# A planned attention and feed-forward kernel: loads and turns dealt out by a clock of the transfers, and the last products in other banks

## The chip, the cores and the metric

The kernel runs on one core of one Trainium2 chip. The metric is the device time of one execution in microseconds (us). The engines are named as in the profile: PE is TensorE (matmuls), PEld its weight loads, DVE is VectorE, ACT is ScalarE, POOL is GpSimd, SP is SyncE, which only issues transfers; ACT and POOL can issue them too. PSUM, where matmuls write, has eight banks.

## What is computed

```python
# q: (8, 16, 384, 64)   k, v: (8, 4, 384, 64)   w_in: (1024, 2048)   w_out: (2048, 1024)
k, v = repeat(k, 4, axis=1), repeat(v, 4, axis=1)
scores = q @ k.T / sqrt(64)
attn = exp(scores - max(scores)); attn = attn / (sum(attn) + 1e-9)
x = (attn @ v).transpose(0, 2, 1, 3).reshape(8 * 384, 1024)
out = (maximum(x @ w_in, 0) ** 2) @ w_out                  # (3072, 1024), float32
```

Grouped-query attention over eight batches feeds a feed-forward layer with a squared ReLU. One batch of attention gives the 384 rows of `x` on which the feed-forward of that batch works.

## The kernel before

The whole kernel is written by a planner that runs when the program is built. The class `Recorder` takes every operation with its engine, what it reads and writes, and a cost in us, and keeps a planned clock for each engine (`R.clock`) and a planned end for each operation. Two loops then choose, step by step, the next piece of work for TensorE among the candidates (`sc` scores, `av` attention times values, `ffn` the next piece of the feed-forward, `top` small products that spread a maximum). The first loop runs until the feed-forward reaches batch `SB` = 2, the second one (batches 2 to 7) to the end. Nothing is decided on the chip: each engine gets its list in the order in which the planner recorded it, with semaphore waits for what the list needs.

The feed-forward of batch b runs beside the attention of batches b+1 and b+2. From batch 2 on, both matrix products are done by Strassen's scheme with seven products in place of eight. The up-projection is in `strassen` (matmuls of 192 columns, L921); its operands are sums of quarters of `x`, made by `sums` on VectorE (L676, four additions of 16-bit values for a batch, kept in the queue `lazy`). The results are drained by `evict` (L892 to L905), and `close_squares` squares them on ScalarE or GpSimd (L806 to L818). The output products are in `products` and `pair_of` (matmuls of 512 columns, L963); their operand sums are in `sum_ops` (L1201), the drains in `copied` and `added` (L1114 and L1121), and one sum of two results is taken on GpSimd (L1153). Pieces that use half of the rows of the array are laid side by side with `zipped`, so two matmuls of 64 rows run at a time. The list of banks for these pieces is `order`, which starts as `[4, 5, 6, 7]` and is permuted by each batch; attention uses banks 0 to 3. `strassen(b)` is built the first time that `whole(b)` is called.

Around TensorE's choice stands `upkeep(now)`, called before every choice. It hands out the work of the other engines in a written order of queues. What the change touches:

- `load_pieces`: the loads of keys and of four groups of query heads for a batch (L292, L327), issued by GpSimd.
- `chores`: per batch the doubling of the keys (`dup_k`, L356: on ScalarE when no list of feed-forward pieces is open, otherwise on GpSimd), the turn of the keys by a transposing transfer (`turn_k_half`, L373), the load of the values (L320), the turns of the queries (`turn_q_dma`, L380) and a copy of the values (`aug_v`, L362).
- `o_wait`: the turns of attention's output into `xT` (`turn_o_dma`, L553). All turns are issued by SP.
- `puts`: the output transfers (`send`, L1329), issued by SP.
- `lazy`, `d_q`, `wide_q`, `calm`, `w2_q`: operations of VectorE and others.

Loads and turns are paced: `dma_at` is the earliest planned time for the next one (`LOAD_GAP` = 2.0 us behind a load, `TURN_GAP` = 3.5 us behind a turn), and `calm_at(now)` looks at the count of matmuls so far, `R.tally.n`: with 128 matmuls to a block and an edge at count 51 of each, it lets a transfer go when the next edge is at least 1.5 us away and the last one at least 0.3 us behind, or when TensorE takes under 18 matmuls a us. Each paced transfer also waits on the chip for the latest matmul recorded before it (`gate`), so that it isn't issued early.

The last output product of the last batch, `whole_product`, is cut in two pieces of 384 and 128 columns; the last drain is split the same way, and `send` puts both on SP's queue.

Of the kernel before, what the change touches and what calls it, by code (L numbers as in the profile page):

```python
# [21 lines left out]
class Recorder:  # L22


    ENGINES = ("tensor", "scalar", "vector", "gpsimd", "sync")
    IN_ORDER = ("tensor",)

    def __init__(self, nc):
        self.nc = nc
        self.ops = []  # L30
        self.writer = {}
        self.readers = {}
        self.dma_sems = {}
# [5 lines left out]
        self.marks = []  # L39

    def deps_of(self, reads, writes):
        deps = set()
# [18 lines left out]
    def add(self, eng, fn, reads=(), writes=(), dma=None, cost=0.1, issue=0.1, shared=(), after=(), port=False):  # L61
        i = len(self.ops)
        deps = self.deps_of(reads, writes)
        raw = {self.writer[r] for r in reads if r in self.writer}
        for r in reads:
            self.readers.setdefault(r, []).append(i)
        for w in writes:
            self.writer[w] = i
            self.readers[w] = []
        need = set(after)  # L70
        for d in deps:
            o = self.ops[d]
            if o["dma"] is None and o["eng"] == eng and dma is None:
                if eng in self.IN_ORDER or d not in raw:
                    continue
            need.add(d)
        if dma is not None:
            if dma in self.dma_last:
                need.add(self.dma_last[dma])
            self.dma_last[dma] = i  # L80
        start = max([self.clock[eng]] + [self.ops[d]["end"] for d in need])
        if dma is not None:
            self.clock[eng] = start + issue
            if eng == "gpsimd":
                self.pool.append((start, start + 0.3 * issue))
            q = eng
            begin = max(self.ring.get(q, 0.0), start + issue + 0.8)
            if shared and begin > start + issue + 0.8:
                shared = (3.0, shared[1])
            if shared and self.ring.get("gpsimd", 0.0) > begin:  # L90
                self.ring["gpsimd"] += shared[1]
                for o in self.ops:
                    if o["eng"] == "gpsimd" and o["dma"] is not None and o["end"] > begin:
                        o["end"] += max(0.0, min(shared[1], o["end"] - 1.2 - begin))
                cost = shared[0]
            self.ring[q] = begin + cost
            end = begin + cost + (1.5 if begin > 30 else 1.2 if eng == "gpsimd" else 0.7)
        else:
            if eng == "gpsimd":
                self.pool.append((start, start + cost))  # L100
            elif port:
                cost += max([0.0] + [z - start for a, z in self.pool[-6:] if a <= start < z])
            self.clock[eng] = start + cost
            if eng == "tensor":
                fn(self.tally)
                self.marks.append((start + cost, self.tally.n))
            end = start + cost + (0.2 if eng == "tensor" else 0.07)
        self.ops.append(dict(eng=eng, fn=fn, dma=dma, need=need, signal=False, start=start, end=end))
        return i
# [57 lines left out]
def bass_gqa_attention__then__ffn_squared_relu_kernel(  # L167
# [12 lines left out]
    B, H, S, D = 8, 16, 384, 64  # L180
# [4 lines left out]
    NKC = F // 128  # L185
# [1140 lines left out]
    def send(b, i3, c0, c1, yb, y0=0):  # L1326
        ysl = y_sb[yb][:, y0:y0 + c1 - c0]
        rows = out[b * S:(b + 1) * S, :].rearrange("(p j) f -> j p f", j=NJ)[i3]
        put = lambda: R.add("sync", lambda e: e.dma_start(rows[:, c0:c1], ysl),  # L1329
                            reads=[("y", yb)], writes=[("out", b, i3, c0)], dma=f"y{yb}" + "z" * (y0 > 0), cost=0.6)  # L1330
# [108 lines left out]
    def prepare(b):  # L1439
# [4 lines left out]
        def go(turn, *args):  # L1444
            turn(b, *args, gate=tuple(pe_last) if paced else ())
            if paced:
                dma_at[0] = R.clock["tensor"] + TURN_GAP
            if turn is turn_q_dma:
                turned_h.add((b, args[0]))
            if turn is turn_q_dma and args == (1,):  # L1450
# [150 lines left out]

    def whole(b):
        if b not in built:
            built[b] = strassen(b, ff["carry"])
        return built[b]

# [37 lines left out]

    BLOCK, EDGE = 128, 51

    def calm_at(now):
        if ff["b"] < SB:
            return True
        n = R.tally.n  # L1650
        t, m = next((x for x in reversed(R.marks) if x[1] <= n - BLOCK // 2), R.marks[0])
        rate = (n - m) / (now - t)
        if rate < 18:
            return True
        left = (EDGE - n) % BLOCK / rate
        return 1.5 <= left <= BLOCK / rate - 0.3

    o_wait = []

    def turn_o_waiting():  # L1660
        while o_wait:
            b, g = o_wait.pop(0)
            turn_o_dma(b, g, tuple(pe_last))
            dma_at[0] = max(dma_at[0], R.clock["tensor"] + 3.5)
            x_done[b] += 2

    def upkeep(now):
        nonlocal loaded, queued, turned
        pe_last[0:1] = [len(R.ops) - 1 - next(i for i, o in enumerate(reversed(R.ops)) if o["eng"] == "tensor")]
        if o_wait and calm_at(now):  # L1670
            turn_o_waiting()
        if loaded + 1 < B and turned >= loaded and not turn_q and not load_pieces and not chores:
            loaded += 1
# [16 lines left out]
            else:  # L1690
# [5 lines left out]
        if load_pieces and now >= dma_at[0] and calm_at(now) and R.when(writes=load_pieces[0][0], reads=(load_pieces[0] + ((),))[2], eng="none") + 2.0 <= now:  # L1696
            load_pieces.pop(0)[1](tuple(pe_last[0:1]))
            dma_at[0] = now + LOAD_GAP
        if not chores and halves and (halves[0] - 1, NU - 1, 5) in scored and (halves[0] > LATE or x_done[halves[0] - 1] == NKC):
            prepare_rest(halves[0])  # L1700
        if not chores and not load_pieces and not halves and queued < loaded and (queued - (queued == 1), NU - 1 if queued + 1 < LATE else NU // 2 - 1, 5) in scored and pairs >= queued * 8 + 8 * (queued == 1) - 8 * (queued + 1 >= LATE):
            queued += 1
            prepare(queued)
        stretch[0] = split and ff["b"] < SB or bool(ff["now"])
        while chores and R.when(reads=chores[0][0], eng="none") + (chores[0] + (False, 0.0))[3 if len(chores[0]) > 3 else -1] <= now + margin and not (len(chores[0]) > 2 and chores[0][2] and (now < dma_at[0] or not calm_at(now))):
            chores.pop(0)[1]()
            if not chores and not halves:
                turned = queued
# [307 lines left out]
```

## Time and profile before

| | |
|---|---|
| Time, median of 3 runs | 399.15 us (398.44 to 399.24) |
| Profiled execution | 397.95 us, span 396.0 us |
| TensorE clock granted | 1.000 |
| TensorE busy | 388.1 us (98%), 7022 matmuls |
| VectorE busy | 316.3 us (80%) |
| ScalarE busy | 264.4 us (67%) |
| GpSimd busy | 151.1 us (38%) |
| Transfers | 44.39 MB, mean 112 GB/s |

The span runs from the first to the last instruction of the profiled execution; the time of that execution is 1.95 us longer. In the rows below, a time such as 298.76 is the start in us from the start of the span, the number behind it the duration; brackets give the idle time ahead of the instruction and what ended it. Line numbers are those of the kernel before; from the edits on, the changed kernel's are up to 13 higher.

### The profile page before, as it was taken

What the parts mean: (1) busy time and instruction counts of PE and PEld (TensorE: products, weight loads), DVE (VectorE), ACT (ScalarE), POOL (GpSimd) and SP (SyncE); (2) the same over time, 40 slices, a digit from 0 to 9 for tenths busy, and PEclk for the clock granted to TensorE, in tenths of its full rate; (3) what the DMA queues carried; (4) which work ended last, traced back from release to release, by engine and by line L of the source; (5) the groups of instructions that cost most, each with busy time, mean ns of one, the idle gap of its engine ahead of it and who ended that gap; (6) DMA issues with size and microseconds to landing.
All of it is one profiled execution on the core that took longest, in us unless ns stands there. A gap on an engine that the chain in (4) does not pass through costs nothing.

```text
span 396.0 us, 15645 instructions
## 1 busy us (share of the span) xinstructions
PE 388.1 (98%) x7022; PEld 292.1 (74%) x7022; DVE 316.3 (80%) x654; ACT 264.4 (67%) x384; POOL 151.1 (38%) x173
## 2 busy tenths in 40 slices
PE   8999999999999999999999999999999999999996
PEld 5565764455655998499876899799974799789653
DVE  3689879899989998878997888878897688856642
ACT  6948999688556796578728587868725597426511
POOL 8656410056002565068413263066420145126111
PEclk9999999999999999999999999999999999999999
DMA  9999999995229936659469957484476221120022
GB/s 171 175 199 187 207 186 192 180 221 82 41 77 141 163 49 83 109 123 102 64 112 190 139 89 73 89 149 58 65 107 167 79 45 25 46 84 3 28 81 106
DMA packets 95634, 44.39 MB, mean 112 GB/s; under 512 B 75984, under 2 KB 89552, under 8 KB 95568
## 3 DMA queue, kind: packets, MB, share of 16 engines
q0 software_dynamic: 36672, 17.44, 35.4%
q1 hardware_dynamic: 58224, 25.47, 32.1%
q8 instruction: 55, 0.90, 0.9%
q10 hardware_dynamic: 672, 0.49, 0.4%
q14 instruction: 11, 0.09, 0.1%
HBM read 35.65 MB, written 12.58 MB: 122 GB/s over the span
## 4 chain that ended last, share of the span: by engine, by line
PE 87%; DVE 7%; DMA 3%; POOL 1%; issue 1%; ACT 0%; ACTq 0%; DVEq 0%
PE ps L963 30%; PE ps L921 27%; PE ps L629 7%; PE ps L466 7%; PE ps L533 7%; PE ps L1297 5%; DMA wx<-in_q_dram 2%; PE ps L492 2%; DVE hr L642 1%; PE ps L592 1%; DMA wx<-in_k_dram 1%; DVE w_out_sb L1247 1%; DVE y_sb L1121 1%; DVE w_out_sb L1259 1%; DVE s_all L676 0%
## 5 line engine op out<-in xcount | busy, mean ns | idle before, releaser
L476 ACT ACTIVATE expT<-ps 128x1024 bf16<-128x1024 f32 (+1 forms) x124 | 121.1, 1017 | 37.6 <-PE ps L466 37.2
L963 PE MATMUL ps<-w_out_sb,h2T 64*128 64x512 f16 x528 | 96.3, 376 | 0.0
L921 PE MATMUL ps<-xT,w_in_sb 64*128 64x192 f16 x1152 | 84.2, 243 | 0.4 <-DVE y_sb L1121 0.3
L921 PEld LDWEIGHTS ps<-xT,w_in_sb 64*128 64x128 f16 x1152 | 71.4, 94 | 3.4 <-DVE y_sb L1121 0.5
L818 POOL TENSOR_TENSOR h2T<-hr 128x384 f16<-128x384 f32 x56 | 45.4, 832 | 45.6 <-ACT hr L806 45.4
L963 PE MATMUL ps<-area,xT 64*128 64x512 f16 x288 | 55.3, 376 | 0.0
L963 PEld LDWEIGHTS ps<-w_out_sb,h2T 64*128 64x128 f16 (+1 forms) x528 | 38.5, 94 | 19.0 <-ACT h2T L814 0.5
L921 PE MATMUL ps<-s_all,wx 64*128 64x192 f16 x768 | 51.8, 243 | 0.0
L466 PE MATMUL ps<-qT,kT 64*128 64x256 bf16 (+2 forms) x336 | 50.3, 323 | 0.9 <-ACT expT L476 0.6
L806 ACT ACTIVATE hr<-hr,bits 128x384 f32<-128x384 f32 x71 | 41.9, 608 | 10.1 <-DVE hr L905 9.5
L921 PEld LDWEIGHTS ps<-s_all,wx 64*128 64x128 f16 x768 | 44.4, 94 | 0.7
L905 DVE TENSOR_TENSOR hr<-ps,hr 128x384 f32<-128x384 f32 x72 | 39.2, 554 | 6.3 <-PE ps L921 2.5
L533 PE MATMUL ps<-v_aug,expT 64*128 64x65 bf16 x1680 | 43.9, 190 | 0.1
L1121 DVE SCALAR_TENSOR_TENSOR y_sb<-ps,bits,y_sb 128x512 f32<-128x512 f32 (+2 forms) x38 | 27.1, 723 | 20.4 <-PE ps L963 9.6
L629 PE MATMUL ps<-xT,w_in_sb 64*128 64x384 bf16 x448 | 41.9, 323 | 1.0 <-DVE hr L642 0.9
L533 PEld LDWEIGHTS ps<-v_aug,expT 64*128 64x128 bf16 x1680 | 39.9, 94 | 1.4 <-PE ps L533 0.2
L1114 ACT ACTIVATE y_sb<-ps,bits 128x512 f32<-128x512 f32 x20 | 13.6, 687 | 35.4 <-PE ps L963 35.4
L963 PE MATMUL ps<-area,h2T 64*128 64x512 f16 x144 | 36.2, 376 | 0.0
L1153 POOL TENSOR_TENSOR y_sb<-y_sb 128x512 f32<-128x512 f32 x9 | 11.9, 1320 | 62.7 <-DVE y_sb L1121 62.7
L629 PEld LDWEIGHTS ps<-xT,w_in_sb 64*128 64x128 bf16 x448 | 21.9, 94 | 16.2 <-DVE hr L642 2.2
L921 PE MATMUL ps<-xT,wx 64*128 64x192 f16 x384 | 33.0, 243 | 0.2 <-DVE hr L905 0.2
L921 PE MATMUL ps<-s_all,w_in_sb 64*128 64x192 f16 x384 | 32.7, 242 | 0.0
(147 smaller groups left out, 748.5 us busy)
## 6 DMA issues: line engine op xcount, KB each, us to landing
out_dram<-y_sb SPq DMA_DIRECT2D x45, 256.0 KB, 2.5
w_in_sb<-in_moe_w_in_dram POOLq DMA_DIRECT2D x8, 512.0 KB, 15.2
w_out_sb<-in_moe_w_out_dram POOLq DMA_DIRECT2D x4, 1024.0 KB, 28.4
q_st<-in_q_dram POOLq DMA_DIRECT2D x19, 192.0 KB, 4.9
q_st<-in_q_dram POOLq DMA_DIRECT2D x4, 384.0 KB, 23.5
k_st<-in_k_dram POOLq DMA_DIRECT2D x6, 192.0 KB, 4.5
k_st<-in_v_dram POOLq DMA_DIRECT2D x5, 192.0 KB, 3.8
wx<-in_q_dram POOLq DMA_DIRECT2D x2, 384.0 KB, 9.1
```

Of the source, the lines that this page charges most:

```text
L466: mm = pe.matmul(ps[:, base + x, m * wide:(m + 1) * wide], kT[at(b)][64 * x:64 * x + 64, u, :], q_cols(b, u // NJ, x, c0, c0 + wide))
L476: R.add("scalar", lambda e: e.activation(dst, src, AF.Exp, scale=0.125), reads=keys, writes=[("expT", slot(b, u), t) for u, _, _ in pieces ...
L533: m = pe.matmul(ps[:, p[x], n * DP:n * DP + D + 1], w, v_aug[b % 2][r, g * NJ + j, 0:D + 1], start=(n + j + y == 0), stop=(n + j + y == 2 ...
L629: m = pe.matmul(bank(4 + xs[x])[:, 0:S], w_in_sb[r, kc, c * 128:(c + 1) * 128], xT[b % NXT][r, kc, :], start=(phase < 2 and kc == 0), stop ...
L806: R.add("scalar", lambda e, val=val, to=to: e.activation(val, val, AF.Relu, scale=to), reads=[("hr", r)] + by, writes=[("hr", r)], cost=0. ...
L818: n = R.add(eng, lambda e, dst=dst, two=two: e.tensor_tensor(dst, two, two, ALU.mult), reads=[("hr", r)], writes=keys, cost=0.77 if other ...
L905: R.add("vector", lambda e: e.tensor_tensor(hr[r][:, :], src, hr[r][:, :], ALU.add), reads=[("bank", at), ("hr", r)], writes=[("hr", r)], ...
L921: return lambda pe: pe.matmul(bank(at)[:, f * h:f * h + h], w[r, kc, c:c + 128], m[r, kc, :], start=(prod in (1, 5, 2) and y + f + kc == 0 ...
L963: return lambda pe: pe.matmul(bank(p.at)[:, 0:512], p.a(k, r), p.w(k, r), start=start, stop=stop, skip_group_check=True)
L1114: R.add(eng, lambda e: e.activation(y_sb[y], bank(at), AF.Copy, scale=gs[g]) if eng == "scalar" else e.tensor_scalar(y_sb[y], bank(at), gs ...
L1121: R.add("vector", lambda e: e.scalar_tensor_tensor(y_sb[z][:, c0:c1], bank(at)[:, c0:c1], gs[g], y_sb[y][:, c0:c1], ALU.mult, ALU.add), re ...
L1297: m = pe.matmul(bank(i)[:, 0:n], h2T[:, c, i3 * 128:(i3 + 1) * 128], w_out_sb[:, c, c0:c1], start=(c == 0), stop=(c == NFC - 1))
```

## The change

A second clock, `R.wire`, is kept in `Recorder.add`: for each transfer, by its kind, a lag and an amount of work (`WIRE`; 2.2 and 1.25 us for a kind that isn't listed) are added up, so that it tells when the transfers given out so far are done. `calm_at` gets the kind of the next transfer and lets it go when the work with it would end less than 1.5 us behind the next edge of 128 matmuls, or, right at an edge, when little is under way; where TensorE takes under 18 matmuls a us, when it would end within 6 us. The fixed gaps behind a load and a turn become 0.5 us, and that behind a turn of attention's output 0, from batch 2 on.

`shut(now)` keeps the sums of `lazy` back while VectorE's next planned start falls into a pass of GpSimd. The sums of batch 3 are taken up earlier. For the last batch `order` is set to banks 0 to 3 before `strassen` is built. The last piece of 128 columns is sent from ScalarE's queue.

```diff
+    WIRE = dict(turn_q=(1.6, 1.9), turn_o=(0.8, 1.3), turn_k=(1.3, 1.3), y=(1.8, 0.8))
...
             self.ring[q] = begin + cost
+            kind = dma.rstrip("0123456789z_")
+            lag, work = self.WIRE.get(kind, (2.2, 1.25))
+            self.wire = max(self.wire, start + lag) + work
...
-        put = lambda: R.add("sync", lambda e: e.dma_start(rows[:, c0:c1], ysl),
+        put = lambda: R.add("scalar" if y0 else "sync", lambda e: e.dma_start(rows[:, c0:c1], ysl),
...
-                dma_at[0] = R.clock["tensor"] + TURN_GAP
+                dma_at[0] = R.clock["tensor"] + (TURN_GAP if ff["b"] < SB else 0.5)
...
     def whole(b):
         if b not in built:
+            if b == B - 1:
+                order[:] = [0, 1, 2, 3]
             built[b] = strassen(b, ff["carry"])
...
-    def calm_at(now):
+    def calm_at(now, kind):
         if ff["b"] < SB:
             return True
         n = R.tally.n
         t, m = next((x for x in reversed(R.marks) if x[1] <= n - BLOCK // 2), R.marks[0])
         rate = (n - m) / (now - t)
+        lag, work = R.WIRE.get(kind, (2.2, 1.25))
+        over = max(R.wire, now + lag) + work
         if rate < 18:
-            return True
+            return over <= now + 6.0
         left = (EDGE - n) % BLOCK / rate
-        return 1.5 <= left <= BLOCK / rate - 0.3
+        return (over <= now + left + 1.5 or left < 0.3 and R.wire <= now + 2.0) and left <= BLOCK / rate - 0.3
...
             turn_o_dma(b, g, tuple(pe_last))
-            dma_at[0] = max(dma_at[0], R.clock["tensor"] + 3.5)
+            dma_at[0] = max(dma_at[0], R.clock["tensor"] + 0)
...
+    def shut(now):
+        t = max(now, R.clock["vector"])
+        return ff["b"] >= SB and any(a <= t < z - 0.3 for a, z in R.pool[-6:])
...
-        if o_wait and calm_at(now):
+        if o_wait and calm_at(now, "turn_o"):
...
-            dma_at[0] = now + LOAD_GAP
+            dma_at[0] = now + (LOAD_GAP if ff["b"] < SB else 0.5)
...
-        while lazy and R.when(reads=lazy[0][0], eng="none") <= now + near and R.clock["vector"] <= now + near:
+        while lazy and R.when(reads=lazy[0][0], eng="none") <= now + near and R.clock["vector"] <= now + near and not shut(now):
...
-        if b and R.when(reads=[("xT", b % NXT, c) for c in range(NKC)], eng="none") + (3.3 if b > SB else 2.0) <= now + 0.3:
+        if b and R.when(reads=[("xT", b % NXT, c) for c in range(NKC)], eng="none") + (3.3 if b > SB + 1 else 1.0 if b > SB else 2.0) <= now + 0.3:
```

Since the planner chooses by its clocks, the lists of all engines come out in another order from batch 2 on. The matmuls are the same 7022, shape by shape. The start of TensorE's list, up to the first pieces of batch 2's up-projection, is unchanged.

More of the change, by code (lines that the diff above doesn't have):

```diff
@@ L39, in __init__ @@
         self.marks = []
+        self.wire = 0.0
     def deps_of(self, reads, writes):
@@ L1695, in upkeep @@
                     load_pieces.append(([("v_st", 0)], lambda g: load_v(n, g)))
-        if load_pieces and now >= dma_at[0] and calm_at(now) and R.when(writes=load_pieces[0][0], reads=(load_pieces[0] + ((),))[2], eng="none") + 2.0 <= now:
+        if load_pieces and now >= dma_at[0] and calm_at(now, "q") and R.when(writes=load_pieces[0][0], reads=(load_pieces[0] + ((),))[2], eng="none") + 2.0 <= now:
             load_pieces.pop(0)[1](tuple(pe_last[0:1]))
-            dma_at[0] = now + LOAD_GAP
+            dma_at[0] = now + (LOAD_GAP if ff["b"] < SB else 0.5)
         if not chores and halves and (halves[0] - 1, NU - 1, 5) in scored and (halves[0] > LATE or x_done[halves[0] - 1] == NKC):
@@ L1704, in upkeep @@
         stretch[0] = split and ff["b"] < SB or bool(ff["now"])
-        while chores and R.when(reads=chores[0][0], eng="none") + (chores[0] + (False, 0.0))[3 if len(chores[0]) > 3 else -1] <= now + margin and not (len(chores[0]) > 2 and chores[0][2] and (now < dma_at[0] or not calm_at(now))):
+        while chores and R.when(reads=chores[0][0], eng="none") + (chores[0] + (False, 0.0))[3 if len(chores[0]) > 3 else -1] <= now + margin and not (len(chores[0]) > 2 and chores[0][2] and (now < dma_at[0] or not calm_at(now, "turn_q"))):
             chores.pop(0)[1]()
```

## The prediction

> **What bounds the kernel now.** I read the head of the page first, then the chain, then the waits of TensorE, and last the timeline at each wait.
>
> ```profile
> span 396.0 us, 15645 instructions
> PE 388.1 (98%) x7022; PEld 292.1 (74%) x7022; DVE 316.3 (80%) x654; ACT 264.4 (67%) x384; POOL 151.1 (38%) x173
> PE 87%; DVE 7%; DMA 3%; POOL 1%; issue 1%; ACT 0%; ACTq 0%; DVEq 0%
> ```
>
> TensorE is busy for 388.1 of 396.0 us and holds 87% of the chain that ended last. Its list is the same 7022 matmuls in the changed program, of the same shapes, counted line by line. So the change can win only what TensorE idles, and the tail behind its last matmul; it can lose any amount. All planner edits are switched by `ff["b"] >= SB`, so they act once the feed-forward is at batch 2, from about 129 us. The waits of TensorE between 129 and 396 us, as total, times and longest:
>
> ```profile
> PE ps L963 <- DVE y_sb L1121: 0.6, 1, 0.6
> PE ps L921 <- DVE y_sb L1121: 0.3, 1, 0.3
> PE ps L466 <- ACT expT L476: 0.3, 1, 0.3
> PE ps L921 <- DVE hr L905: 0.2, 1, 0.2
> ```
>
> That is 1.4 us in four waits, and no releaser is a transfer. Hence the part that gives the change its name, earlier loads and turns, has no wait on TensorE to remove in this execution. What can be won hangs on VectorE's order.
>
> One correction. A matmul row outlasts the step to the next pair:
>
> ```profile
> L963 PE MATMUL ps<-w_out_sb,h2T 64*128 64x512 f16 x528 | 96.3, 376 | 0.0
> 156.13 5.18 PE ps L963 x48
> ```
>
> 48 half-array matmuls in 5.18 us are 24 pairs of 0.216 us each, while one row lasts 0.376. So a stall has eaten 0.16 us of lost pace before a gap shows: each wait above costs its idle time plus 0.16.
>
> **The change part by part.** First, sums out of GpSimd's passes. The largest wait, with what ran ahead of it on VectorE and GpSimd:
>
> ```profile
> 292.13 1.16 POOL L362 COPY v_aug<-k_st 128x768 bf16<-128x768 bf16 x1 [2.85 <-DMA k_st<-in_v_dram]
> 292.53 1.18 DVE L676 TENSOR_TENSOR s_all<-xT 128x768 f16<-128x768 f16 x1
> 295.30 0.74 DVE L1121 SCALAR_TENSOR_TENSOR y_sb<-ps,bits,y_sb 128x512 f32<-128x512 f32 x1
> 295.96 0.54 DVE L676 TENSOR_TENSOR xT<-xT 128x768 f16<-128x768 f16 x1
> 296.12 1.51 POOL L1153 TENSOR_TENSOR y_sb<-y_sb 128x512 f32<-128x512 f32 x1 [2.83 <-DVE y_sb L1121]
> 296.42 1.62 DVE L676 TENSOR_TENSOR s_all<-xT,s_all 128x768 f16<-128x768 f16 x1
> 297.97 0.74 DVE L1121 SCALAR_TENSOR_TENSOR y_sb<-ps,bits,y_sb 128x512 f32<-128x512 f32 x1
> 298.76 0.39 PE L963 MATMUL ps<-w_out_sb,area 64*128 64x512 f16 x1 [0.63 <-DVE y_sb L1121]
> ```
>
> The add at 296.42 lasts 1.62 us where its like lasts 0.54. It began inside GpSimd's pass, which ends at 297.63, and ends 0.41 behind it at 298.04; the add at 292.53 does the same against the pass that ends at 293.29. The add at 295.96 began 0.16 us ahead of the pass and kept its length. So an add that starts inside a GpSimd pass waits the pass out. The drain at 297.97 stands behind it, and TensorE waits for that drain's bank. In the changed order only one of the four sums stands between the two drains, not two: the lists read drain, add, add, drain before and add, drain, add, drain after. GpSimd's pass starts on the first drain's end, so the one add left begins ahead of it, as that of 295.96 did. The two lists hold the same four operations, so the second drain gains the stretch, 1.62 - 0.54 = 1.08 us, more than the 0.79 (0.63 + 0.16) that TensorE lost. Next late is the first drain, which now has an add of 0.54 ahead of it; its row shows no wait of a matmul behind it. I take the whole stall, **-0.79**; between 0 and -0.79.
>
> The Trainium skill, "SBUF — State Buffer", section "Who interferes with whom", says that a VectorE instruction with two SBUF inputs and a GpSimd instruction that reads SBUF block each other fully, whichever issues second waiting to the end. The three adds agree with that. By this rule GpSimd's own pass is held instead when the add is first; the trace has that too, 1.51 us at 296.12, and only an output transfer follows it.
>
> Second, the same collision with a copy that is moved.
>
> ```profile
> 136.79 1.46 POOL L356 COPY k_dup<-k_st 128x1536 bf16<-128x1536 bf16 x1
> 137.23 1.56 DVE L1259 TENSOR_TENSOR w_out_sb<-w_out_sb 128x1024 f16<-128x1024 f16 x1
> 138.72 1.01 DVE L905 TENSOR_TENSOR hr<-ps,hr 128x384 f32<-128x384 f32 x2
> 139.31 0.25 PE L921 MATMUL ps<-xT,wx 64*128 64x192 f16 x1 [0.24 <-DVE hr L905]
> L1259 DVE TENSOR_TENSOR w_out_sb<-w_out_sb x4: 677/1160/1559, 134.1 to 141.3; 128x1024 f16<-128x1024 f16 x4
> ```
>
> Here 1.56 us against a least of 0.68. The changed order puts this operation one drain of attention (reciprocal and multiply) earlier, so that the reciprocal and the multiply stand between it and the adds of L905. Whether the copy still meets it the order does not tell; between 0 and -0.40 (0.24 + 0.16), I take **-0.40**, because the adds of L905 no longer stand directly behind the long operation.
>
> Third, the last products in attention's banks (`order[:] = [0, 1, 2, 3]` for the last batch).
>
> ```profile
> 349.33 1.41 DVE L1121 SCALAR_TENSOR_TENSOR y_sb<-ps,bits,y_sb 128x512 f32<-128x512 f32 x2 [1.46 <-PE ps L921]
> 350.14 1.50 PE L921 MATMUL ps<-xT,w_in_sb 64*128 64x192 f16 x32 [0.28 <-DVE y_sb L1121]
> ```
>
> The first products of the last batch stop for a bank that a drain of the batch before still reads. Attention's banks 0 to 3 are long empty then. The drain of 349.33 stays but nobody waits for it: 0.28 + 0.16 = **-0.44**; next late there would be the vector sums, which stand before it in the list. I see little that takes it back.
>
> Fourth, the tail. The last piece of 128 columns goes out on ScalarE's queue instead of second on SP's.
>
> ```profile
> 393.08 0.35 DVE L1121 SCALAR_TENSOR_TENSOR y_sb<-ps,bits,y_sb 128x128 f32<-128x128 f32 x1
> 393.45 0.82 SPq L1329 DMA_DIRECT2D out_dram<-y_sb  x2
> out_dram<-y_sb SPq DMA_DIRECT2D x1, 192.0 KB, 1.9
> out_dram<-y_sb SPq DMA_DIRECT2D x1, 64.0 KB, 1.8
> L1329 SPq DMA_DIRECT2D out_dram<-y_sb x47: 332/333/1243, 75.7 to 393.8; - x47
> ```
>
> Both wait for the add that ends at 393.43. The 192 KB piece lands 1.9 us after 393.45, at 395.35; the 64 KB piece, issued 0.33 to 0.38 later, at about 395.6. Side by side, the first sets the end: **-0.25**; between 0 and -0.38. ScalarE has nothing behind that issue.
>
> Fifth, loads and turns by the transfer clock. No wait of TensorE is theirs, so nothing is taken out. What moves: four query loads in a row on GpSimd (they stood two, one, one between squares), turns of queries, keys and outputs back to back on SP, output transfers behind them. On GpSimd the squares wait behind up to four issues; SP's output transfers wait too, but y buffers come round after tens of us. Two key copies move from GpSimd to ScalarE, which is 67% busy:
>
> ```profile
> L1114 ACT ACTIVATE y_sb<-ps,bits 128x512 f32<-128x512 f32 x20 | 13.6, 687 | 35.4 <-PE ps L963 35.4
> L356 POOL COPY k_dup<-k_st 128x1536 bf16<-128x1536 bf16 x4 | 6.1, 1516 | 0.0
> PE ps L629 <- DVE hr L642: 0.9, 2, 0.7
> ```
>
> A copy of 1.5 us ahead of an exponential that TensorE needs could cost that much at worst. But the code gives it to ScalarE only outside a running list of pieces, among output products, and there ScalarE sat idle for 35.4 us behind L963 (the row of L1114), so I put it at nothing. But re-dealing the order of six batches will make some new wait. The nearest price is one small wait, 0.20 + 0.16 = **+0.36**; from 0 to two waits like the longest one of TensorE, 2 × (0.7 + 0.16) = 1.72.
>
> Sum: -0.79 - 0.40 - 0.44 - 0.25 + 0.36 = **-1.5**. The profiled execution took 397.95 us (1.95 around its span of 396.0), so 396.45; the median of the runs is 399.15, 1.2 above it, and by the same difference comes out at 397.65. I forecast **397.7**. A change within 0.2%, 0.8 us, is about what cannot be told from none.
>
> **The rivals.** *New waits take back what the old ones gave.* For it: VectorE is 80% busy, four small waits go and the order behind each is new, and the price above reaches 1.72. Against it: the two largest gains have a cause that is gone by construction (bank, add count). Then -1.88 + 1.72, about -0.2: 399.0, no difference.
>
> *Clumped turns delay TensorE's instructions; slower.* The page's queues:
>
> ```profile
> q0 software_dynamic: 36672, 17.44, 35.4%
> q1 hardware_dynamic: 58224, 25.47, 32.1%
> q8 instruction: 55, 0.90, 0.9%
> xT<-o_sb SPq DMA_TRANSPOSE x26, 3.1
> qT<-q_st SPq DMA_TRANSPOSE x12, 4.7
> kT<-k_dup SPq DMA_TRANSPOSE x11, 3.4
> 221.00:226.00 5.00, 5.00 (x175) 4.86 (x171) 4.73 (x10) 2.69 (x4) 0.67 (x1) 1.00 0.89 130
> ```
>
> 55 transfers bring 7022 matmuls and as many weight loads: one for 128 pairs. Each takes 0.9% × 16 × 396 / 55 = 1.04 us on one engine. At 175 matmuls in 5 us TensorE eats a block in 3.7 us, so a block that is late by over 3.7 - 1.0 = 2.7 us stops it. After the change output, key and query turn stand in a row three times, which never happened before; one behind the other they last 3.1 + 3.4 + 4.7 = 11.2 us. Against it: in 221 to 226 us a key turn, three output transfers, an output turn and a query load's tail overlapped, and TensorE was busy for 5.00 of 5.00. If a block waits out just what a query turn has over that block, 4.7 - 3.7 = 1.0, and the 1.04 of its own, three clumps cost 6.1 at worst and 3.1 with half: 397.65 + 3.1 = 400.8, slower. It decides from 2.7 us of delay.
>
> The Trainium skill, "DMA: Bandwidth & Descriptors", section "Queues, rings and completion order", has each DMA engine go round its queues packet by packet. By that rule a block waits for a packet or two of the others and never for a clump, and this rival is worth nothing; it would equally leave the transfer clock without use.
>
> **How the numbers follow.** The forecast, faster by more than 0.8 us, gets 0.68: three of four gains are seen in rows, and each alone is under the bound, so two must come. No difference gets 0.15. Slower gets 0.17: the clumps with most of it, the ScalarE copy with the rest. The forecast's own range goes from 396.0 (all gains, no new wait, -1.88, and some 1.2 for the runs lying nearer to the profiled one) to 398.3; with the same case and part of the slower one it reaches 400.4, and about one in ten lies beyond.
>
> **What would show it.** Right: in the waits of TensorE after 129 us the row with L963 behind the drain is gone, no L921 waits for a drain near 349 us, no sum of the last but one batches lasts over 1 us, and the last two transfers are issued side by side. Wrong: a new releaser of TensorE of over 0.5 us (an exponential behind a key copy, a drain behind a stretched sum), or steps with no releaser named in the stretches where turns stand three in a row, which would be its instructions. If all waits are gone and the time is the same, then the runs' 1.2 us above the profiled one hold something that this page does not show.

## The result and the profile after

| | before | after |
|---|---|---|
| Time, median | 398.88 us (398.00 to 400.00) | 396.16 us (395.66 to 397.23) |
| Profiled execution, span | 397.95 us, 396.0 us | 397.23 us, 395.4 us |
| First row of the stretch to the start of the last matmul | 129.77 to 392.55: 262.78 us | 130.92 to 391.92: 261.00 us |

The ratio of the times is 0.9935 (0.9913 to 0.9958): faster by 2.7 us. In the runs of the experiments the changed kernel took 395.68 us beside 397.99 before, 0.9937 (0.9918 to 0.9957). The last row of the table is the part that the change touches, from the first L921 (after: L926) behind a pair of scores to the start of the last matmul. The list of TensorE up to there is the same in both, and only its position in the span differs from execution to execution: this first row lay between 128.6 and 131.0 us in the profiles below. So comparisons of two traces go by this stretch. It is 1.78 us shorter.

The page after, its span and first part:

```profile
span 395.4 us, 15642 instructions
PE 388.7 (98%) x7019; PEld 295.8 (75%) x7022; DVE 312.0 (79%) x649; ACT 270.6 (68%) x394; POOL 144.7 (37%) x168
```

Three matmul records are missing from this trace, and from all those below; the 7022 weight loads are there. The waits of TensorE between 129 and 396 us (total, times, longest), where there were four with 1.4 us:

```profile
PE ps L471 <- DVE bits L712: 0.2, 1, 0.2
PE ps L926 <- DVE y_sb L1126: 0.2, 1, 0.2
```

The timeline of VectorE and GpSimd at the place where the longest wait was, now with one sum between the two drains:

```profile
296.99 0.55 DVE L681 TENSOR_TENSOR xT<-xT 128x768 f16<-128x768 f16 x1
297.61 0.75 DVE L1126 SCALAR_TENSOR_TENSOR y_sb<-ps,bits,y_sb 128x512 f32<-128x512 f32 x1
298.28 0.55 DVE L681 TENSOR_TENSOR s_all<-xT,s_all 128x768 f16<-128x768 f16 x1
298.44 1.51 POOL L1158 TENSOR_TENSOR y_sb<-y_sb 128x512 f32<-128x512 f32 x1 [13.31 <-DVE y_sb L1126]
299.55 0.75 DVE L1126 SCALAR_TENSOR_TENSOR y_sb<-ps,bits,y_sb 128x512 f32<-128x512 f32 x1 [0.73 <-PE ps L968]
```

The sum at 298.28 is ahead of the pass and keeps 0.55 us. The second drain now waits for TensorE (0.73 behind L968), not the other way round. One sum of another batch still meets a pass, the copy of L1225 that ends at 255.84, and ends 0.43 behind it:

```profile
254.27 2.00 DVE L681 TENSOR_TENSOR s_all<-xT 128x768 f16<-128x768 f16 x1
```

### The profile page after: what moved, and what is told of

Its sections match the earlier page's. It is cut to its first block, busy times and chain, and to the rows that moved or that the text cites. A ratio compares the mean times of both kernels' runs of the same rounds, so it can differ in the third digit from the quotient of the medians.

```text
span 395.4 us, 15642 instructions
## 1 busy us (share of the span) xinstructions
PE 388.7 (98%) x7019; PEld 295.8 (75%) x7022; DVE 312.0 (79%) x649; ACT 270.6 (68%) x394; POOL 144.7 (37%) x168
## 5 line engine op out<-in xcount | busy, mean ns | idle before, releaser
L968 PE MATMUL ps<-w_out_sb,h2T 64*128 64x512 f16 x528 | 98.1, 376 | 0.0
L926 PE MATMUL ps<-xT,w_in_sb 64*128 64x192 f16 x1152 | 83.8, 243 | 0.3 <-DVE y_sb L1126 0.2
L926 PEld LDWEIGHTS ps<-xT,w_in_sb 64*128 64x128 f16 x1152 | 70.7, 94 | 3.0 <-PE ps L926 0.7
L823 POOL TENSOR_TENSOR h2T<-hr 128x384 f16<-128x384 f32 x54 | 43.5, 826 | 55.6 <-ACT hr L811 55.6
L968 PE MATMUL ps<-area,xT 64*128 64x512 f16 x288 | 55.7, 376 | 0.0
L968 PEld LDWEIGHTS ps<-w_out_sb,h2T 64*128 64x128 f16 (+1 forms) x528 | 39.1, 94 | 17.7 <-ACT h2T L819 0.3
L471 PE MATMUL ps<-qT,kT 64*128 64x256 bf16 (+2 forms) x336 | 51.2, 327 | 0.6 <-ACT expT L481 0.4
L926 PE MATMUL ps<-s_all,wx 64*128 64x192 f16 x768 | 51.3, 242 | 0.0
L926 PEld LDWEIGHTS ps<-s_all,wx 64*128 64x128 f16 x768 | 44.1, 94 | 1.0
L538 PE MATMUL ps<-v_aug,expT 64*128 64x65 bf16 x1680 | 42.7, 190 | 0.0
L538 PEld LDWEIGHTS ps<-v_aug,expT 64*128 64x128 bf16 x1680 | 38.9, 94 | 1.5
L1119 ACT ACTIVATE y_sb<-ps,bits 128x512 f32<-128x512 f32 x23 | 15.6, 687 | 34.9 <-PE ps L968 34.7
L1158 POOL TENSOR_TENSOR y_sb<-y_sb 128x512 f32<-128x512 f32 x9 | 11.9, 1320 | 67.4 <-DVE y_sb L1126 67.4
L968 PE MATMUL ps<-area,h2T 64*128 64x512 f16 x144 | 35.9, 376 | 0.0
L634 PEld LDWEIGHTS ps<-xT,w_in_sb 64*128 64x128 bf16 x448 | 21.1, 94 | 16.8 <-DVE hr L647 2.2
L926 PE MATMUL ps<-xT,wx 64*128 64x192 f16 x384 | 32.9, 242 | 0.0
L926 PE MATMUL ps<-s_all,w_in_sb 64*128 64x192 f16 x384 | 32.2, 242 | 0.0
```

The source lines that it names most:

```text
L471: mm = pe.matmul(ps[:, base + x, m * wide:(m + 1) * wide], kT[at(b)][64 * x:64 * x + 64, u, :], q_cols(b, u // NJ, x, c0, c0 + wide))
L538: m = pe.matmul(ps[:, p[x], n * DP:n * DP + D + 1], w, v_aug[b % 2][r, g * NJ + j, 0:D + 1], start=(n + j + y == 0), stop=(n + j + y == 2 ...
L634: m = pe.matmul(bank(4 + xs[x])[:, 0:S], w_in_sb[r, kc, c * 128:(c + 1) * 128], xT[b % NXT][r, kc, :], start=(phase < 2 and kc == 0), stop ...
L823: n = R.add(eng, lambda e, dst=dst, two=two: e.tensor_tensor(dst, two, two, ALU.mult), reads=[("hr", r)], writes=keys, cost=0.77 if other ...
L926: return lambda pe: pe.matmul(bank(at)[:, f * h:f * h + h], w[r, kc, c:c + 128], m[r, kc, :], start=(prod in (1, 5, 2) and y + f + kc == 0 ...
L968: return lambda pe: pe.matmul(bank(p.at)[:, 0:512], p.a(k, r), p.w(k, r), start=start, stop=stop, skip_group_check=True)
```

## The experiments

Times "before" beside each group come from the same chip. The theory (A): VectorE's place in the order decides, through sums that wait out a pass of GpSimd; loads and turns are hidden. Its rival (B): the transfer clock itself is worth the time, or takes it.

### The transfer clock alone

```diff
 # the kernel before, with only:
+    WIRE = dict(turn_q=(1.6, 1.9), turn_o=(0.8, 1.3), turn_k=(1.3, 1.3), y=(1.8, 0.8))
+            self.wire = max(self.wire, start + lag) + work
...
 # calm_at(now, kind) and the gaps of 0.5 and 0 as in the change
```

> The kernel before with the transfer clock alone (its account of transfers, the new test ahead of loads and turns, the short gaps); sums, banks and the last transfer as before. Measure inside the trace: from the first matmul of batch 2's up-projection to the end of the span, 266.2 us in the kernel before (129.77 to 396.0) and 264.5 in the changed one (130.92 to 395.4). Theory A (the gain is a handful of VectorE waits, the transfers themselves were hidden): the wait for the drain ahead of the last batch (0.28 us idle) and the serial last transfer (0.25) stay; the new order may lose or gain others; 265 to 266.5 in this measure and under 1.5 us of gain in time. Theory B (transfers dealt out better are worth time that the waits of one trace do not show, because 2.7 us are gained in time and 1.7 in the trace): 264.5 to 265 and 1.5 us or more of gain in time.

403.07 us beside 397.99: ratio 1.0124 (1.0085 to 1.0163), slower by 5.1 us, more than any price of a single wait in the traces so far. Both theories missed: neither expected such a loss. The waits of TensorE behind 129 us, and the row of the longest:

```profile
PE ps L926 <- DVE y_sb L1126: 4.2, 3, 3.8
175.68 2.74 PE L926 MATMUL ps<-xT,w_in_sb 64*128 64x192 f16 x32 [3.77 <-DVE y_sb L1126]
```

One stop of 3.77 us ahead of 175.68, 3.93 with the lost pace. The timeline ahead of it, VectorE and GpSimd:

```profile
165.17 2.96 POOL L332 DMA_DIRECT2D q_st<-in_q_dram  x4 [0.16 <-issue]
168.24 1.26 POOL L1158 TENSOR_TENSOR y_sb<-y_sb 128x512 f32<-128x512 f32 x1
168.69 1.23 DVE L681 TENSOR_TENSOR s_all<-xT 128x768 f16<-128x768 f16 x1
169.45 2.21 POOL L1225 COPY area<-h2T 128x2048 f16<-128x2048 f16 x1
169.95 2.13 DVE L681 TENSOR_TENSOR s_all<-s_all,xT 128x768 f16<-128x768 f16 x1
171.61 1.79 POOL L361 COPY k_dup<-k_st 128x1536 bf16<-128x1536 bf16 x1
172.00 1.81 DVE L681 TENSOR_TENSOR xT<-xT 128x768 f16<-128x768 f16 x1
174.88 1.40 DVE L1126 SCALAR_TENSOR_TENSOR y_sb<-ps,bits,y_sb 128x512 f32<-128x512 f32 x2
```

Three passes stand back to back on GpSimd, behind four query loads that it now issues in a row. Each of three sums of batch 3 ends 0.41 to 0.42 us behind a pass (169.92 behind 169.50, 172.08 behind 171.66, 173.81 behind 173.40): 5.17 us instead of 1.65. The drain at 174.88, which frees the bank for TensorE, stands behind them. The stop is followed by something that costs three quarters as much again. The windows (PE, PEld, DVE, ACT, POOL busy, then the granted clock):

```profile
171.92:174.89 2.97, 0.00 (x0) 0.00 (x0) 2.90 (x7) 0.00 (x0) 1.49 (x1) 1.00 0.41 106
174.89:175.68 0.79, 0.00 (x0) 0.00 (x0) 0.79 (x3) 0.00 (x0) 0.00 (x0) 0.50 0.00 0
175.68:181.72 6.04, 6.04 (x86) 5.39 (x88) 3.35 (x8) 2.01 (x4) 0.00 (x0) 0.50 0.42 119
181.72:185.00 3.28, 3.28 (x102) 3.15 (x98) 2.77 (x8) 2.00 (x4) 2.36 (x3) 1.00 0.61 45
```

The granted clock falls to 0.50 at 174.89, when TensorE has been idle for 3.0 us, and is 1.00 again from 181.72. So 6.04 us of work run at half the clock, which costs 3.0. With the 3.93 that is 6.9, and the stretch, 268.31 us, is 6.87 longer than in the kernel below that differs from this one by one constant (261.44). The Trainium skill, "TensorE: Matmul & The Clock Gate", section "Part 1: The HAM clock gate (the "warmup" mystery)", says that TensorE falls to half its clock after an idle window of about 3.4 us. The trace agrees in the main: a stop of 3.8 us did it here, though the clock fell 3.0 us into it, and one of 2.5 us did not (below). The same section has the full clock back after a busy window of about 3.4 us, in windows that run on regardless of the kernel; here the half clock lasted 6.83 us, two such windows, and the first still held 0.8 us of idle time.

### All of the change but the transfer clock

```diff
 # the kernel before, with the tail on ScalarE's queue, the banks of the last batch,
 # shut(now) and the early sums (3.3 to 1.0); calm_at, dma_at and the gaps as before
```

> The changed kernel without the transfer clock: loads and turns keep the old test and the old gaps; sums, banks and the last transfer are changed. Theory A: the three places go whose cause is changed here, the stretched sum near 298 us (0.79), the bank ahead of the last batch (0.44) and the tail (0.25); the wait near 139 us stays (0.40), since the list there is that of before; 264.7 to 265.2 in the stretch from the first matmul of batch 2's up-projection to the end, 1.0 to 1.5 us of gain in time. Theory B: under 1 us of gain in time, the rest is the clock's.

398.80 us, ratio 1.0010 (0.9993 to 1.0028): no difference, where theory A expected a gain of 1.0 to 1.5 us. Its waits of TensorE, and the row of the last:

```profile
PE ps L963 <- DVE y_sb L1121: 0.5, 1, 0.5
PE ps L921 <- DVE hr L905: 0.2, 1, 0.2
PE ps L921 <- issue: 0.2, 1, 0.2
232.08 0.24 PE L921 MATMUL ps<-xT,wx 64*128 64x192 f16 x1 [0.21 <-issue]
```

The stall at 350 us is gone (0.44 with the lost pace) and that at 298 has shrunk from 0.79 to 0.12; that at 139 stays (0.40), and two new ones take 0.63 and 0.37. The stretch is 262.45 us, 0.33 under before, and the tail behind the last add takes 2.91 us, 0.33 more than before. This is the prediction's first rival, new waits for old ones, as it happens. The new wait of 0.37, at 232.08, has no releaser; a block of TensorE's instructions began its transfer 2.42 us ahead of it, at 229.66. What that means comes out at the kernel with a gap of 1.0 us. Theory B's number, a gain under 1 us, was met, but its reason, that the transfer clock is worth the rest, was not: alone the clock costs 5.1 us.

### The change with its edges turned round

```diff
-        return (over <= now + left + 1.5 or left < 0.3 and R.wire <= now + 2.0) and left <= BLOCK / rate - 0.3
+        return left <= 1.0 or left >= BLOCK / rate - 0.3
```

> The changed kernel with the test turned round: in the fast stretches a load or a turn goes only within 1.0 us ahead of an edge of 128 matmuls or 0.3 us behind one, with no account of what is under way. Theory A and the rule that each transfer engine goes round its queues packet by packet: the block of instructions is not held up, no pause of TensorE over 0.2 us without a releaser; any loss is a named wait for a transfer that comes late (turns and output transfers now lie closer, up to 3 us at one place). Rival (clumps starve TensorE of instructions): pauses of 0.5 us or more with no releaser at several of the places where turns stand in a row, 2 to 6 us in all.

400.98 us, ratio 1.0066 (1.0043 to 1.0090). The stop that costs most, in the timeline and with its clock:

```profile
167.23 2.91 DVE L681 TENSOR_TENSOR s_all<-xT,s_all 128x768 f16<-128x768 f16 x1
167.81 1.91 POOL L1225 COPY area<-h2T 128x2048 f16<-128x2048 f16 x1
171.66 0.74 DVE L1126 SCALAR_TENSOR_TENSOR y_sb<-ps,bits,y_sb 128x512 f32<-128x512 f32 x1
172.55 0.24 PE L926 MATMUL ps<-xT,w_in_sb 64*128 64x192 f16 x1 [2.45 <-DVE bits L696]
172.50:175.00 2.50, 2.39 (x95) 2.30 (x97) 2.50 (x3) 0.00 (x0) 1.84 (x2) 1.00 0.16 30
```

The sum again ends 0.42 behind a pass (170.14 behind 169.72), though its record starts 0.58 ahead of it; the drain at 171.66 stands behind it, and TensorE goes on 0.15 after that drain's end. The row names L696, which came last on VectorE. The clock stays at 1.00. So most of the time was lost behind a sum (2.61 of 3.99 us in the stretch, with the lost pace). The pauses without a releaser of 0.5 us or more that the rival expected did not come; the one wait of that kind is 0.3 us at 136.79. In this order, turns at the edges didn't starve TensorE.

### The changed kernel again

> The changed kernel once more, for what one profile differs from the next. The list up to batch 2 is the same in all kernels here, so the start of batch 2's up-projection (129.77 us in the one profile before, 130.92 in the one after) tells what the opening alone varies by. Theory A: the stretch from there to the end repeats within 0.2 us of 264.5, and the opening varies by 1 us. Otherwise (the opening is slower for a reason of the change): 130.9 again.

395.68 us. The stretch is 260.97 us where the first trace had 261.00, so differences of 0.1 us in it can be read. It begins at 130.70, near the 130.92 of the first trace; but in other kernels with the same list up to there it begins at 128.6 to 131.0 (129.34 in the one with the banks of before), so the opening varies by itself.

### The transfer clock alone, with GpSimd's passes made short

```diff
-        R.add(eng, lambda e: e.copy(dst, src) if eng == "scalar" else e.tensor_copy(dst, src),
+        R.add(eng, lambda e: e.copy(dst, src) if eng == "scalar" else e.tensor_copy(dst[:, 0:1], src[:, 0:1]) if b > 2 else e.tensor_copy(dst, src),
...
-                R.add("gpsimd", lambda e: e.tensor_tensor(y_sb[z], y_sb[z], y_sb[y], ALU.add),
+                R.add("gpsimd", lambda e: e.tensor_tensor(y_sb[z][:, 0:32], y_sb[z][:, 0:32], y_sb[y][:, 0:32], ALU.add),
...
 # the copy of L1225 whole on ScalarE at no planned cost, and one of its rows on GpSimd
```

> The kernel before with the transfer clock alone, as in the first experiment, and the long passes of GpSimd made short with TensorE's, VectorE's and SP's lists unchanged: the sum of two products (L1158) on 32 of 512 columns, the doubling of the keys (L361, those that GpSimd does from batch 3 on) on one of twelve rows, the copy of a third of the squares (L1225) done by ScalarE. It leaves out most of those two results. Theory A (a sum of batch 3 that starts inside a pass of GpSimd waits the pass out, and TensorE stands behind the drain after it): the sums take 0.55 us each instead of 1.23, 2.13 and 1.81, so 3.5 us less; of TensorE's stop of 3.93 near 175 us some 0.4 is left, the granted clock stays at 1.00 there, which gives another 3.4; time about 396, and at most 397.5. Rival (the turns and loads that stand in a row hold TensorE or its instructions, and the stretched sums are only beside it): the stop stays above 2 us and the time above 400.

395.44 us beside 397.96, ratio 0.9939 (0.9917 to 0.9961), against 403.07 with the passes. The same place in the timeline of GpSimd, and one of the four kinds of sum over the whole run (least, median, longest ns; the others lie between 540 and 559):

```profile
165.83 0.24 POOL L1158 TENSOR_TENSOR y_sb<-y_sb 128x32 f32<-128x32 f32 x1
170.31 0.29 POOL L1226 COPY area<-h2T 128x128 f16<-128x128 f16 x1 [4.24 <-ACT area L1225]
170.54 0.29 POOL L361 COPY k_dup<-k_st 128x128 bf16<-128x128 bf16 x1
L681 DVE TENSOR_TENSOR s_all<-s_all,xT x6: 548/558/559, 124.6 to 341.6; 128x768 f16<-128x768 f16 x6
```

Loads, turns and the order on TensorE and VectorE are those of the first experiment, and the stop and the half clock are gone. So the passes made them, not the transfers. Of the stop 0.24 us is left (0.40 with the lost pace), at 169.74 for the same drain. The stretch is 261.48 us, and the changed kernel's 261.00 with the bank (0.44), that rest (0.40) and without the wait at 260.13 (0.37) makes 261.47. That wait is in the first experiment too (0.19 us, at 267.04, behind a sum held to 1.99 us) and is gone here: so 0.37 us is what GpSimd's passes still cost the changed kernel.

### The transfer clock and the early sums of batch 3

```diff
 # the kernel of the first experiment, and:
-... + (3.3 if b > SB else 2.0) <= now + 0.3:
+... + (3.3 if b > SB + 1 else 1.0 if b > SB else 2.0) <= now + 0.3:
```

> The kernel before with the transfer clock and the early sums of batch 3 (3.3 to 1.0), and nothing else: banks, tail and guard as before. TensorE's list is that of the changed kernel. Theory A (the sums of batch 3 are all that was wrong with the transfer clock alone): no stop near 175 us, no sum over 1 us there, granted clock 1.00; the time is that of the changed kernel plus the bank (0.44), the tail (0.25) and at most 0.3 near 298, so 396.4 to 397.0. Rival (the changed kernel needs its guard as well, or the banks do more than one wait): over 398.

396.35 us, ratio 0.9958 (0.9944 to 0.9973), just under the 396.4 to 397.0 that A expected. One constant is worth 6.7 us here (403.07 to 396.35). The timeline shows where the sums went:

```profile
163.45 2.97 POOL L332 DMA_DIRECT2D q_st<-in_q_dram  x4 [0.16 <-issue]
164.38 0.55 DVE L681 TENSOR_TENSOR s_all<-xT 128x768 f16<-128x768 f16 x1
166.58 0.55 DVE L681 TENSOR_TENSOR s_all<-xT,s_all 128x768 f16<-128x768 f16 x1
166.75 1.50 POOL L1158 TENSOR_TENSOR y_sb<-y_sb 128x512 f32<-128x512 f32 x1 [0.33 <-DVE y_sb L1126]
```

They stand beside GpSimd's issues of loads, ahead of its passes. The stretch is 261.44 us, the changed kernel's and 0.44: the bank alone. The guard `shut` adds nothing that can be seen.

### The changed kernel with the banks of before

```diff
-            if b == B - 1:
-                order[:] = [0, 1, 2, 3]
```

> The changed kernel without the bank order for the last batch. By the prediction's term the wait of L926 for a drain near 349 us is back, 0.28 idle and 0.16 of lost pace: 0.44 in the stretch from 130 us to the end, so the time of the changed kernel plus 0.4, which this measurement can hardly tell from none; the wait in the trace can. Rival (the drain is early enough in the new order): no such wait, and the stretch is the same within 0.1.

396.30 us, ratio 0.9963 (0.9946 to 0.9979); the stretch 261.44 us, again 0.44 over the changed kernel, and the waits:

```profile
PE ps L926 <- DVE y_sb L1126: 0.5, 2, 0.3
PE ps L471 <- DVE bits L712: 0.2, 1, 0.2
```

The second wait for a drain is back, at 348.38 us. The term of the prediction holds within the 0.03 us by which the stretch repeats.

### The changed kernel with a gap of 1.0 us behind a load

```diff
-            dma_at[0] = now + (LOAD_GAP if ff["b"] < SB else 0.5)
+            dma_at[0] = now + (LOAD_GAP if ff["b"] < SB else 1.0)
```

> The changed kernel with a gap of 1.0 us instead of 0.5 behind a load from batch 2 on: loads of queries less close together, and with them another order of the list from the first third on. Theory A (transfers are hidden, VectorE's order decides): the same as the changed kernel, within 0.8 us, and what differs is a wait for a drain of VectorE. Rival (loads in a row cost TensorE time): faster by over 0.8 us.

398.07 us, ratio 0.9992 (0.9969 to 1.0015): the whole gain is gone, and both theories missed. Its waits, and the timeline of TensorE at the first:

```profile
PE ps L926 <- issue: 1.5, 1, 1.5
PE ps L926 <- DVE y_sb L1126: 0.8, 1, 0.8
175.34 0.24 PE L926 MATMUL ps<-s_all,wx 64*128 64x192 f16 x2
177.10 0.73 PE L926 MATMUL ps<-s_all,wx 64*128 64x192 f16 x13 [1.52 <-issue]
```

The second wait is A's: a sum of 2.74 us at 256.35, which ends 0.42 behind the copy of L1225. The first has no releaser, and it falls inside eight matmuls of which only the first waits for anything in the list. What comes late there is the block of instructions. Its transfer begins at 174.66 us, when 2749 matmuls have begun, in the changed kernel's two traces at 2685 and 2654. The transfers of this kernel from 168 to 174.6 us:

```profile
q0 software_dynamic: 1869, 0.69, 98.5%
q1 hardware_dynamic: 266, 0.50, 21.0%
q14 instruction: 1, 0.01, 0.3%
```

There is no q8, the queue that brings TensorE's blocks, and the packets of q0, GpSimd's loads, add up to 98.5% of the 16 engines' time (with q1 it is over 100, so packets overlap). So a third theory (C): a clump of transfers holds the block up, and TensorE runs out of instructions. Three more kernels with the same lists tested it.

### The gap of 1.0 us with short query loads, with short output transfers, and again

```diff
 # short query loads
-            q_st[st][:, h0:h1, :],
-            q[b, h0:h1].rearrange("h (p j) d -> p h (j d)", j=NJ)),
+            q_st[st][:, h0:h0 + (1 if b > 3 else h1 - h0), :],
+            q[b, h0:h0 + (1 if b > 3 else h1 - h0)].rearrange("h (p j) d -> p h (j d)", j=NJ)),
 # short output transfers, from batch 2 on
-        put = lambda: R.add("scalar" if y0 else "sync", lambda e: e.dma_start(rows[:, c0:c1], ysl),
+        put = lambda: R.add("scalar" if y0 else "sync", lambda e: e.dma_start(rows[:, c0:c1 - (c1 - c0) * 7 // 8 * (b > 1)], ysl[:, 0:c1 - c0 - (c1 - c0) * 7 // 8 * (b > 1)]),
```

> The kernel with the gap of 1.0 us, with the loads of queries from batch 4 on cut to one of their four heads; all lists stay in their order. It leaves out three quarters of those queries. In the kernel with the gap TensorE stopped for 1.5 us at 177.10, in the middle of eight matmuls that wait for nothing, and the transfer of one instruction block began at 174.66, at matmul 2749, where four other kernels have it at 2641 to 2685. Theory C (the block waited behind transfers that stand close together, and TensorE ran out of instructions): with the queue of GpSimd's loads short, the block comes by matmul 2690, the stop is gone, the stretch from the first matmul of batch 2's up-projection to the last one falls from 263.2 to 261.5 us, and the time to about 396.4. Theory A (VectorE's order alone): the stop at 177 stays, over 1.0 us, and the time stays near 398.

> The kernel with the gap of 1.0 us, with the output transfers from batch 2 on cut to an eighth of their columns; all lists stay in their order. It leaves out seven eighths of those outputs. Theory C says that some of the transfers that ran from 169 to 174.7 us held the block: if it was the three output transfers issued at 169.00 to 171.75, the block comes by matmul 2690 here, the stop is gone and the time is about 396.4 or, with the tail's transfers short too, 396; if it was GpSimd's loads, the stop stays. Theory A: the stop stays over 1.0 us.

> The kernel with the gap of 1.0 us once more. If the stop at 177 us comes from the lists, it is there again with 1.5 us give or take 0.3, and the block's transfer begins at matmul 2740 or later; if it was an accident of one execution, it is gone.

| | time | block's transfer begins, us | matmuls begun | behind matmul 2663 | lost at the stop |
|---|---|---|---|---|---|
| short query loads | 396.10 (0.9959; 0.9932 to 0.9986) | 171.47 | 2663 | 0 | 0 |
| short outputs | 395.75 (0.9944; 0.9926 to 0.9963) | 173.40 | 2730 | 2.28 us | 1.19 us |
| the gap | 398.07 | 174.66 | 2749 | 2.69 us | 1.68 us |
| the gap again | 397.94, one execution | 173.79 | 2753 | 2.91 us | 1.74 us |

The column "behind matmul 2663" says how much later the block's transfer begins than at that matmul, where it begins with short query loads.

With short query loads the stop is gone, the stretch falls from 263.21 to 261.41 us, and the transfers of the same 6.6 us show the block:

```profile
q1 hardware_dynamic: 428, 0.78, 33.4%
q0 software_dynamic: 288, 0.10, 14.6%
q8 instruction: 1, 0.02, 1.7%
```

With short outputs the stop is smaller but there. So the delay needs GpSimd's loads, and the outputs lengthen it by 0.4 to 0.6 us: C holds. A's first half, that transfers are hidden, is false in this kernel and true in the changed one, where no stop of TensorE behind 129 us lacks a releaser. It is false, in small, in two kernels with the old pacing as well. The wait at 232.08 in the kernel with all but the clock stands 2.42 us behind the beginning of a block's transfer, as the stops here stand 2.3 to 2.4 behind theirs. And in the kernel before the weight loads have a gap with no releaser 2.45 us behind a block that began at 267.97:

```profile
270.42 0.09 PEld L921 LDWEIGHTS ps<-xT,wx 64*128 64x128 f16 x1 [0.20 <-issue]
```

TensorE loses 0.13 us there. That these two are late blocks is read from the times alone; no run took the transfers away.

With short outputs the median is lower than its profiled execution, 397.05, whose stretch is 262.74. The tail is 0.57 us shorter there, since the last transfers are short too; why its executions differ by up to 2.2 us stays open.

## Why the prediction was right, point by point

It forecast 397.7 us from 399.15, 1.45 less; measured were 2.7 and 2.3 less, in the trace 1.78. The way and three of the terms are right; the size is in part luck, as the points on the tail and on the transfer clock show.

- **Sums out of GpSimd's passes, -0.79: held.** The stall at 298 is gone in the way described. Its cause was a matter of order and not of the guard: it is gone too in the kernel without `shut`.
- **The copy that met L1259, -0.40: held, by other means.** The operation now starts 0.14 ahead of the copy and keeps its length, and the copy takes longer:

```profile
137.39 0.74 DVE L1264 TENSOR_TENSOR w_out_sb<-w_out_sb 128x1024 f16<-128x1024 f16 x1
137.53 1.93 POOL L361 COPY k_dup<-k_st 128x1536 bf16<-128x1536 bf16 x1
```

- **Banks, -0.44: held**, with 0.44 measured in two kernels.
- **The tail, -0.25: wrong.** From the end of the last add to the end of the span it takes 2.58 us before and 2.62 after. In the experiments with full outputs it takes 2.57 and 2.58 with the old tail, and 2.61 to 2.64 with the new one (2.91 in the kernel with all but the clock): the edit costs some 0.04 us. The step that failed let the last 64 KB land in the same 1.8 us on the other queue; beside the 192 KB they take 2.2:

```profile
392.84 0.37 ACTq L1334 DMA_DIRECT2D out_dram<-y_sb  x1
out_dram<-y_sb SPq DMA_DIRECT2D x1, 192.0 KB, 2.0
out_dram<-y_sb ACTq DMA_DIRECT2D x1, 64.0 KB, 2.2
```

- **One small new wait, +0.36: one came, 0.37**, at 260.13 for a drain. Two stalls that the prediction didn't price went as well: 0.22 at 155.67 and 0.13 at 270.42. In sum -0.79 - 0.40 - 0.44 - 0.22 - 0.13 + 0.37 is -1.61; the last 0.17 wasn't traced to any one stall.
- **The transfer clock at nothing but that wait, bounded by 1.72: mis-sized.** Alone it costs 5.1 us. The prediction priced a stall by its neighbours in the trace and had none that also halves the clock. And the early sums of batch 3, which it named in no term, are what keeps this from happening: here the forecast held by luck. The parts don't add up: the clock alone +5.1, the rest alone +0.8 with an interval that holds zero, together -2.3.
- **The first rival** came true in the kernel without the transfer clock. The second, clumps that starve TensorE, didn't happen in the changed kernel: the longest transfer of a block behind 125 us took 1.81 us there and 1.67 before. But its mechanism is real, with the wrong transfers and the wrong threshold. Query loads on GpSimd make it, not turns, and it decides from 1.0 to 1.2 us of delay (2.69 - 1.68, 2.28 - 1.19, 2.91 - 1.74), not from 2.7; in the kernel with short passes the same block was 0.96 us late and nothing stopped. The step that failed let a block be used when its 1.0 us of transfer were over; TensorE went on 2.3 to 2.4 us after the transfer's start.
- **The page against it**, "DMA: Bandwidth & Descriptors", section "Queues, rings and completion order", of the Trainium skill, has each DMA engine change queues packet by packet, by which the prediction let a block wait for a packet or two and never for a clump. That doesn't explain the gap kernel, where the block began 2.7 us late and came in time once the loads were short. Whether it stood in its queue or was asked for late no trace shows.
- **From the profiled execution to the median: wrong.** The prediction took the median to lie 1.2 us above the profiled execution, as before. After the change it lies 1.07 below (396.16 and 397.23): the two profiled executions differ by only 0.72 us, since the stretch begins 1.15 later in the second.

Between the traces' 1.8 us and the medians' 2.3 and 2.7 stay 0.5 to 0.9 us, inside the intervals. The part ahead of 130 us, whose list is the same, moves by more than that between executions; which share is whose wasn't settled.

## What to carry to other kernels

When a reordering touches several engines, look in the new order for two-input operations of VectorE that will start beside a pass of GpSimd with a drain behind them: here that one thing moved the time by 6.7 us, and transfers moved it only where they delayed instructions. Parts of such a change can't be priced one by one, since each is tuned to the order that the others make; build the pairs. And read a wait of TensorE that has no releaser against the queue that brings its instructions: a late block is as good a cause as a late operand.

## What the hardware showed that was not expected

- A stop of 3.8 us on TensorE halved its clock for the 6.0 us of work behind it, so it cost 1.8 times its length (3.93 and 3.0); one of 2.5 us left the clock at 1.00.
- A sum whose record starts 0.42 or 0.58 us ahead of GpSimd's copy of L1225 still ends 0.42 behind it (259.09 behind 258.67; 170.14 behind 169.72), while a sum 0.16 ahead of the pass of L1158 keeps 0.55 us. Being first in the records is no protection against the copy.
- A late block of TensorE's instructions began its transfer 2.3 to 2.4 us before its first matmul, and with GpSimd's loads adding up to 98.5% of the DMA engines' time it began 2.7 us late.
